# Attention and two expert layers on one core: the first query chunk's blocks go to TensorE's transposes, and the round gets a new order

## Chip, cores and metric

One core of a Trainium2 chip runs the kernel. The metric is device time in microseconds (us) of one execution; smaller is better. The kernel before took 905.91 us, the median of three runs (905.5 to 911.83).

## What is computed

Three layers follow one another. The first is causal attention over 4 batches of 12 heads, 448 tokens, 64 features a head. Then come two layers that send each of the 1792 tokens to one of 8 experts; they are not touched by the change.

```python
scores = scale * np.matmul(q, k.transpose(0, 1, 3, 2))
mask = np.triu(np.ones((seq, seq), dtype=bool), k=1)
scores = np.where(mask, -1000000000.0, scores)
scores = scores - np.max(scores, axis=-1, keepdims=True)
attn = np.exp(scores)
attn = attn / (np.sum(attn, axis=-1, keepdims=True) + 1e-09)
return np.matmul(attn, v).astype(np.float32)
```

## The kernel before

**Tiles.** Attention goes over 24 pairs of heads. The 448 tokens are cut into four chunks of 112 (`CP`), and because of the causal mask query chunk c needs key chunks 0 to c only: 1 + 2 + 3 + 4 = 10 blocks of 112x112 a head (`NB`). For the product with the values a block must stand with its keys on the partitions, so every block of exponentials is transposed.

**Stages of a pair.** `qk` writes the mask and the scores of two query chunks for both heads into four banks of PSUM (`sc`). `rowmax` on DVE finds the maximum of a row (`nm`), `expo` on ACT writes the exponentials to `ex`. Blocks are then split in two halves of 16 bits: `hi` is the block in fp16, `lo` what that leaves over. Two ways lead from there.

- The six blocks of chunks 0, 1 and 2 (`ND`) are split first: `halves_hi` writes `ah` on ACT, `halves_lo` writes `al` on DVE. Then the queue of SP transposes them by DMA into `th` and `tl`, one `DMA_TRANSPOSE` a head and half, four a pair.
- The four blocks of chunk 3 are transposed in fp32 by TensorE into the bank `tb0` (`last_chunk`, one "filling" a head), and split when they are read out of it: ACT writes `ph`, DVE writes `pl`.

`values` multiplies them with the values, which are split in three parts: five products a block, 50 a head, all for one head in a bank `av`, but for one chunk of the second head that goes to `tb1`. `combine` on DVE divides by the sum and writes the result `xb`. `route_t` and `route_l` prepare the choice of experts of the next layer, and a generator of routing steps (`routing`) gives DVE one small step at each `tick`.

**What sets the order.** The program is scheduled by hand: each engine runs its instructions in the order in which the code issues them. The loop over g (L783) is a pipeline; a pass of it, called a round here, works on the scores of pair g, the splits and transposes of pair t = g - 1, the values of pair v = g - 2 and the routing of pair r = g - 3. On the queue of SP a round holds, in this order, the loads of q, k and v of later pairs (L371, L377), two transposes of `tl`, in some rounds a store of `xb`, and two transposes of `th` (all four issued by L421, the helper `transposed`). The transposes of `tl` that a round issues are read by `values` in the next.

In a round TensorE does: scores of chunks 0 and 1, the first filling (head 0), `route_t`, `values(v, 0)`, scores of chunks 2 and 3, the second filling (head 1), `values(v, 1)`, `route_l`.

```python
    boff = [0, 1, 3, 6]
...
    def transposed(dst, src, e):
        nc.sync.dma_start_transpose(dst[:, e * ND * CP : (e + 1) * ND * CP].rearrange("p (n q) -> p n q", q=CP),
                                    src[:, e].rearrange("p n k -> p (n k)"))
```

Of the kernel before, what the change touches and what calls it, by code (L numbers as in the profile page):

```python
# [9 lines left out]
F32 = mybir.dt.float32  # L10
F32R = mybir.dt.float32r
BF16 = mybir.dt.bfloat16
F16 = mybir.dt.float16
# [43 lines left out]
def attention_two_moe_kernel(  # L57
# [258 lines left out]
    NB = NCH * (NCH + 1) // 2  # L316
    ND = NB - NCH
    exs = [at_p.tile([CP, 2, NB, CP], F32, name=f"ex{i}") for i in range(NEX)]
# [4 lines left out]
    phs = [av_p.tile([CP, 2 * NCH * CP + 16], F16, name=f"ph{i}") for i in range(NTP)]  # L323
    pls = [av_p.tile([CP, 2 * NCH * CP + 16], F16, name=f"pl{i}") for i in range(NTP)]
    for t in ahs + als:
        vec.memset(t[:, :, :, CP:], 0.0)
# [5 lines left out]
    for t in phs + pls:  # L332
        vec.memset(t[:, 2 * NCH * CP :], 0.0)


    tb = [ps_t.tile([P, 512], F32, tag="t", name="tb0"), ps_x.tile([P, 512], F32, tag="t2", name="tb1")]

    def side():

        return tb[0][:, S:] if tb else ps_t.tile([P, 512], F32, tag="t", name="t")  # L340

# [49 lines left out]

    boff = [0, 1, 3, 6]
    scs, nms, avs = {}, {}, {}
# [41 lines left out]

    def last_chunk(g, e):

        pt = tb[0][:CP, :S]
        for j in range(NCH):
            pe.transpose(pt[:, j * CP : (j + 1) * CP], exs[g % NEX][:, e, ND + j], ident[:CP, :CP])  # L440
        yield
        ph, pl = (t[g % NTP][:, e * S : (e + 1) * S] for t in (phs, pls))
        act.activation(ph, pt, AF.Copy, scale=ASC)
        yield
        vec.scalar_tensor_tensor(out=pl, in0=pt, scalar=ASC, in1=ph, op0=ALU.mult, op1=ALU.subtract)
        tick()

    VW = HD + 1

    def values(g, e):  # L450

        if e == 1 and g not in tails:
            tails[g] = tb[1][:, S:]
        if e == 0:
            avs[g] = ps_x.tile([P, 512], F32, tag="av", name=f"av{g}")
        v0, v1, v2 = (t[:, e] for t in vss[g])
        for c in range(NCH):
            k = c if e == 0 else NCH + (c - 1) % NCH
            at = k * VW
            for j in range(c + 1):  # L460
                if c < NCH - 1:
                    o = (e * ND + boff[c] + j) * CP
                    hi, lo = (t[g % NTH][:CP, o : o + P] for t in (ths, tls))
                else:
                    o = (e * NCH + j) * CP
                    hi, lo = (t[g % NTP][:, o : o + P] for t in (phs, pls))
                ops = ((hi, v1), (hi, v0), (hi, v2), (lo, v0), (lo, v1))
                for i, (l, r) in enumerate(ops):
                    first, final = j == 0 and i == 0, j == c and i == 4
                    whole = r is v1  # L470
                    if k < 2 * NCH - 1:
                        dst = avs[g][:, at : at + VW] if whole else avs[g][:, at + 1 : at + VW]
                        pe.matmul(dst, lhsT=l, rhs=r[:, j], start=first, stop=final)
                    else:
                        if whole:
                            pe.matmul(avs[g][:, at : at + 1], lhsT=l, rhs=r[:, j, :1], start=first, stop=final)
                        pe.matmul(tails[g], lhsT=l, rhs=r[:, j, 1:] if whole else r[:, j], start=first, stop=final)
# [197 lines left out]
    def both(fn, g, *a, ticks=True):  # L675
        for e in range(2):
            fn(2 * g + e, *a)
            if ticks:
                tick()
# [103 lines left out]
    for g in range(NPR + 3):  # L783
# [12 lines left out]
        if 0 <= v < NPR and v % PB == 0:  # L796
            xbs[v // PB] = xb_p.tile([CP, NCH, D], F32, tag="xb", name=f"xb{v // PB}")
        late = [last_chunk(t, e) if 0 <= t < NPR else iter(()) for e in range(2)]
        if g < NPR:
            qk(g, (0, 1))  # L800
        tick(True)
        if g < NPR:
            for c in range(2):
                both(rowmax, g, c)
                if g == c == 0:
                    both(expo, 0, 0, ticks=False)
                    scale_pair(1, vec)
            for c in range(g == 0, 2):
                both(expo, g, c, ticks=False)
        next(late[0], None)  # L810
        next(late[0], None)
        if 0 <= t < NPR:
            halves_lo(t, (0,))
        next(late[0], None)
        if 0 <= t < NPR:
# [16 lines left out]
        if 0 <= v < NPR:  # L832
            values(v, 0)
        if PB <= r < NPR and r % PB < NCH:
# [8 lines left out]
        if g < NPR:  # L843
            qk(g, (2, 3))
            for c in range(2, NCH):
                both(rowmax, g, c)
        next(late[1], None)
        for c in range(2, NCH):
            if g < NPR:
                both(expo, g, c, ticks=False)  # L850
            next(late[1], None)
        if 0 <= v < NPR:
            values(v, 1)
        if 0 <= r < NPR:
            route_l(r)
        if 0 <= v < NPR:
            combine(v, xbs[v // PB])
        if g < NPR:
            halves_hi(g)
        if g + 2 < NPR:  # L860
            scale_pair(g + 2, pool)
        if g == 0:
# [656 lines left out]
```

## Time and profile before

| what | value |
|---|---|
| median of three runs | 905.91 us |
| the profiled execution | 908.99 us |
| its span, first to last instruction | 907.3 us |
| mean granted TensorE clock | 0.974 of full speed |
| PE busy, share of the span | 848.7 us, 94% |
| DVE busy | 678.2 us, 75% |
| ACT busy | 427.1 us, 47% |
| POOL busy | 399.0 us, 44% |

PE is TensorE's matmuls, PEld its loads of the stationary operand, DVE is VectorE, ACT ScalarE, POOL GpSimd, and SPq the sequencer of SyncE, which issues the DMAs. Shares over the whole span mix three layers with different limits. Attention takes some 250 us at the start, so its stage has to be cut out, and is best cut into rounds. A timeline merges neighbours of one kind: "x4" is four instructions, and the time beside it runs from the first start to the last end. "Idle before" is how long the engine stood in front of an instruction, and behind the arrow is what ended that.

### The profile page before, as it was taken

The page shows a single profiled execution, that of the slowest core. Times are in us where ns is not written, and L with a number is a line of the kernel's source. Part 1 is how long each engine was busy: PE and PEld are TensorE (multiplying, and loading weights), DVE is VectorE, ACT ScalarE, POOL GpSimd, SP SyncE. Part 2 cuts the span into 40 slices and gives each one's busy share as a digit, 9 for nine tenths or more (in the row PEclk, how much of TensorE's full clock was granted, in tenths as well). Part 3 has the DMA queues.
Part 4 walks back from the last instruction along what each step waited for, and adds up shares of the span by engine and source line. Part 5 has one row for each costly group of instructions (what it writes and reads, how often), then busy time and mean ns, then how long its engine had stood idle before and what let it go on. Part 6 is the DMA issues. An engine that isn't in the chain of part 4 may idle for free. (4 is left out here: it accounts for less than half of the span.)

```text
span 907.3 us, 20634 instructions
## 1 busy us (share of the span) xinstructions
PE 848.7 (94%) x6818; PEld 729.4 (80%) x6818; DVE 678.2 (75%) x1782; ACT 427.1 (47%) x777; POOL 399.0 (44%) x433
## 2 busy tenths in 40 slices
PE   5999999988788999999999999999999999999985
PEld 2677776766576899988899989888898898998984
DVE  6888998987876766787747964468786778976783
ACT  4667867775435754575535552245112133221323
POOL 6224245423266264544542564432654544545530
PEclk8899999998799999999999999999999999999997
DMA  7799998998737774687515761120291133511110
GB/s 227 143 160 164 206 199 178 206 174 169 238 97 262 280 260 163 210 290 257 185 46 172 239 229 62 49 73 6 62 328 56 54 108 117 182 43 59 49 38 16
DMA packets 114451, 137.39 MB, mean 151 GB/s; under 512 B 78381, under 2 KB 82787, under 8 KB 114288
## 3 DMA queue, kind: packets, MB, share of 16 engines
q1 hardware_dynamic: 101376, 108.76, 44.4%
q0 software_dynamic: 12912, 26.83, 9.3%
q8 instruction: 57, 0.93, 0.4%
q14 instruction: 106, 0.87, 0.3%
HBM read 101.48 MB, written 19.92 MB: 134 GB/s over the span
## 5 line engine op out<-in xcount | busy, mean ns | idle before, releaser
L748 POOL DMA_INDIRECT xg<-x,xi x128 | 134.4, 1050 | 101.2 <-DMA x<-yb,mg 47.7
L956 PE MATMUL h<-w1h,xh 128*128 128x512 f32 x408 | 164.6, 403 | 2.4 <-issue 1.4
L958 PE MATMUL h<-w1h,xl 128*128 128x512 f32 x408 | 161.1, 395 | 0.9 <-DVE xl L941 0.9
L957 PE MATMUL h<-w1l,xh 128*128 128x512 f32 x408 | 161.2, 395 | 0.7 <-DVE w1l L698 0.7
L1021 PE MATMUL o<-w2h,hh 128*128 128x384 f32 x528 | 137.5, 341 | 0.2 <-issue 0.2
L1021 PE MATMUL o<-w2h,hl 128*128 128x384 f32 x528 | 135.3, 337 | 0.5 <-DVE hl L971 0.5
L1021 PE MATMUL o<-w2l,hh 128*128 128x384 f32 x528 | 134.4, 336 | 0.0
L998 DVE STREAM_TRANSPOSE hs<-h 32x256 f32<-32x256 f32 x240 | 107.1, 446 | 14.3 <-PE h L958 8.5
L418 ACT ACTIVATE ex<-sc,nm 112x112 f32<-112x112 f32 (+1 forms) x192 | 82.8, 499 | 60.9 <-DVE nm L413 58.6
L1021 PEld LDWEIGHTS o<-w2h,hl 128*128 128x128 f32 x528 | 95.3, 188 | 0.8 <-DVE hl L971 0.8
L1021 PEld LDWEIGHTS o<-w2h,hh 128*128 128x128 f32 x528 | 94.0, 188 | 1.8 <-issue 0.4
L1021 PEld LDWEIGHTS o<-w2l,hh 128*128 128x128 f32 x528 | 95.2, 188 | 0.1
L1004 ACT ACTIVATE hh<-hs 128x512 fp32r<-128x512 f32 x30 | 18.4, 631 | 157.7 <-PE o L1021 86.5
L958 PEld LDWEIGHTS h<-w1h,xl 128*128 128x128 f32 x408 | 77.0, 189 | 19.3 <-DVE xl L941 1.6
L956 PEld LDWEIGHTS h<-w1h,xh 128*128 128x128 f32 x408 | 77.2, 189 | 18.8 <-issue 2.3
L957 PEld LDWEIGHTS h<-w1l,xh 128*128 128x128 f32 x408 | 77.3, 189 | 17.9 <-DVE w1l L698 2.6
L413 DVE TENSOR_REDUCE nm<-sc 112x1 f32<-112x112 f32 (+1 forms) x192 | 74.7, 438 | 19.0 <-PE sc L407 18.8
L698 DVE TENSOR_TENSOR w1l<-w1r,w1h 128x1024 fp32r<-128x1024 f32 x66 | 76.4, 1219 | 9.2 <-ACT w1h L696 5.8
L698 DVE TENSOR_TENSOR w2l<-w2r,w2h 128x768 fp32r<-128x768 f32 x78 | 68.8, 951 | 8.6 <-ACT w2h L696 5.6
L407 PE MATMUL sc<-r 64*112 64x112 f32 (+3 forms) x384 | 64.5, 458 | 3.9 <-DVE rt_ren L175 3.9
L696 ACT CAST w1h<-w1r 128x1024 fp32r<-128x1024 f32 x64 | 62.4, 1047 | 9.2 <-PE h L958 5.2
L929 DVE STREAM_TRANSPOSE xr<-xg 128x768 f32<-128x768 f32 x31 | 50.3, 1623 | 17.7 <-DMA xg<-x,xi 11.1
(316 smaller groups left out, 1735.6 us busy)
## 6 DMA issues: line engine op xcount, KB each, us to landing
w1r<-in_w1a SPq DMA_DIRECT2D x48, 512.0 KB
w2r<-in_w2a SPq DMA_DIRECT2D x64, 384.0 KB
r<-in_kqP SPq DMA_DIRECT2D x24, 448.0 KB
w1r<-in_w1b SPq DMA_DIRECT2D x18, 512.0 KB
w2r<-in_w2b SPq DMA_DIRECT2D x24, 384.0 KB
vr<-in_vh SPq DMA_DIRECT2D x24, 224.0 KB
x<-xb SPq DMA_DIRECT2D x16, 336.0 KB
xg<-x,xi POOLq DMA_INDIRECT x128
```

Source lines behind the costliest of these rows:

```text
L407: pe.matmul(scs[2 * g + e, c][:CP, :n], lhsT=r[rs, 1, c * CP : n], rhs=r[rs, 0, :n], start=False, stop=True, skip_group_check=True)
L413: vec.tensor_reduce(out=nms[h][:, c : c + 1], in_=scs[h, c][:CP, : CP * (c + 1)], axis=AX.X, op=ALU.min)
L418: act.activation(dst, scs.pop((h, c))[:CP, :n], AF.Exp, bias=nms[h][:, c : c + 1], scale=-1.0)
L696: act.copy(hi[k], r[k])
L698: vec.tensor_sub(lo[k], r[k], hi[k].bitcast(F32))
L748: pool.indirect_dma_start(out=xgs[j % 3][:, q * (D // Q) : (q + 1) * (D // Q)], out_offset=None, in_=quarters, in_offset=IND(ap=xi[:, q : ...
L929: vec.transpose(xr.rearrange("p k (q r) -> p q k r", q=Q), xgs[j % 3].rearrange("p (q r k) -> p q k r", q=Q, k=KD))
L956: pe.matmul(hps, lhsT=xh[:, c], rhs=w1h[c][:, ns], start=(c == 0), stop=False)
L957: pe.matmul(hps, lhsT=xh[:, c], rhs=w1l[c][:, ns], start=False, stop=False)
L958: pe.matmul(hps, lhsT=xl[:, c], rhs=w1h[c][:, ns], start=False, stop=(c == KD - 1))
L998: vec.transpose(hr[cols, :, rows], hps[rows, q * 256 : (q + 1) * 256].rearrange("p (c k) -> p k c", c=QR))
L1021: pe.matmul(ops[:, n, :384], lhsT=h[f // KH][:, f % KH], rhs=w[f][:, n * 384 : (n + 1) * 384], start=(f == 0 and st == 0), stop=(f == KF - ...
```

## The change

The block of query chunk 0 of each head leaves the DMA's way: `ND` falls from six to five, and the two blocks of a pair (one a head) become a third filling of `tb0`, transposed by TensorE and split out of it into two new small tiles, `qh` (ACT) and `ql` (DVE). `boff` gives the blocks new places, chunks 1 and 2 first, then chunk 0, then chunk 3. `turned_part` takes the place of `last_chunk` and serves all three fillings, and `values` is told which chunks to do and in which order.

The order of a round changes with it:

- The second filling is transposed, copied and split before the scores of chunks 2 and 3 instead of behind them; the third lies behind those scores.
- `values(v, 0)` does chunks 0, 2 and 3 where it stood, and chunk 1 behind the scores of chunks 2 and 3. `values(v, 1)` does chunk 0 last.
- On ACT the copy of the first filling lies between the exponentials of chunk 0 and those of chunk 1.
- `tick(True)` moves from behind the scores of chunks 0 and 1 to behind those of chunks 2 and 3, there is a `tick` more a round, and the routing's small results use the end of `tb1` instead of `tb0`.

```diff
-    ND = NB - NCH
+    ND = NB - NCH - 1
...
+    qhs = [av_p.tile([CP, 2 * CP + 16], F16, name=f"qh{i}") for i in range(NTP)]
+    qls = [av_p.tile([CP, 2 * CP + 16], F16, name=f"ql{i}") for i in range(NTP)]
...
+    for t in qhs + qls:
+        vec.memset(t[:, 2 * CP:], 0.0)
...
-        return tb[0][:, S:] if tb else ps_t.tile([P, 512], F32, tag="t", name="t")
+        return tb[1][:, S:] if tb else ps_t.tile([P, 512], F32, tag="t", name="t")
...
-    boff = [0, 1, 3, 6]
+    boff = [5, 0, 2, 6]
...
-    def last_chunk(g, e):
-
-        pt = tb[0][:CP, :S]
-        for j in range(NCH):
-            pe.transpose(pt[:, j * CP : (j + 1) * CP], exs[g % NEX][:, e, ND + j], ident[:CP, :CP])
-        yield
-        ph, pl = (t[g % NTP][:, e * S : (e + 1) * S] for t in (phs, pls))
+    def turned_part(g, part):
+
+        wide = S if part < 2 else 2 * CP
+        pt = tb[0][:CP, :wide]
+        blocks = [(part, boff[3] + j) for j in range(NCH)] if part < 2 else [(e, boff[0]) for e in range(2)]
+        for k, (e, j) in enumerate(blocks):
+            pe.transpose(pt[:, k * CP : (k + 1) * CP], exs[g % NEX][:, e, j], ident[:CP, :CP])
+        yield
+        at = part * S if part < 2 else 0
+        ph, pl = (t[g % NTP][:, at : at + wide] for t in ((phs, pls) if part < 2 else (qhs, qls)))
         act.activation(ph, pt, AF.Copy, scale=ASC)
         yield
         vec.scalar_tensor_tensor(out=pl, in0=pt, scalar=ASC, in1=ph, op0=ALU.mult, op1=ALU.subtract)
         tick()
+        yield
...
-    def values(g, e):
+    def values(g, e, cs):
...
-        for c in range(NCH):
+        for c in cs:
...
-                if c < NCH - 1:
+                if c in (1, 2):
...
-        tick(True)
-        if g < NPR:
...
-            for c in range(g == 0, 2):
-                both(expo, g, c, ticks=False)
-        next(late[0], None)
-        next(late[0], None)
+            if g:
+                both(expo, g, 0, ticks=False)
+        next(parts[0], None)
+        next(parts[0], None)
+        if g < NPR:
+            both(expo, g, 1, ticks=False)
...
-            values(v, 0)
+            values(v, 0, (0, 2, 3))
+        if v >= 0:
+            drain(parts[1])
...
             qk(g, (2, 3))
+        tick(True)
+        drain(parts[1])
+        if 0 <= v < NPR:
+            values(v, 0, (1,))
+        next(parts[2], None)
+        if g < NPR:
             for c in range(2, NCH):
                 both(rowmax, g, c)
-        next(late[1], None)
-        for c in range(2, NCH):
-            if g < NPR:
-                both(expo, g, c, ticks=False)
-            next(late[1], None)
+            both(expo, g, 2, ticks=False)
+        next(parts[2], None)
+        if g < NPR:
+            both(expo, g, 3, ticks=False)
+        next(parts[2], None)
         if 0 <= v < NPR:
-            values(v, 1)
+            values(v, 1, (1, 2, 3, 0))
```

On PE, in the middle of a round of before, the scores of chunks 2 and 3 (`sc_2`, `sc_3`; one of the four masks is shown) come straight after the last product of `values(v, 0)` with `pl`; the second filling (`tb_253`) comes behind them and in front of `values(v, 1)`:

```order
L473 MATMUL av_1453<-r_236,pl_230 128x65
...
L401 MATMUL sc_2_1504<-mask,identb 128x112
...
L407 MATMUL sc_2_1504<-r_646 112x336
L407 MATMUL sc_2_1506<-r_646 112x336
L407 MATMUL sc_3_1508<-r_646 112x448
L407 MATMUL sc_3_1510<-r_646 112x448
L440 MATMUL tb_253<-ident,ex_215 112x112 x4
L476 LDWEIGHTS th_223
```

Now, at the same place on PE, the second filling (`x4`, into `tb_261`) stands ahead of the scores, and the third (`x2`) behind them and behind chunk 1 of `values(v, 0)`, of which the first and the last product are shown:

```order
L481 MATMUL av_1485<-r_240,pl_230 128x65
L446 MATMUL tb_261<-ident,ex_215 112x112 x4
...
L405 MATMUL sc_2_1532<-mask,identb 128x112
...
L411 MATMUL sc_2_1532<-r_662 112x336
L411 MATMUL sc_2_1534<-r_662 112x336
L411 MATMUL sc_3_1536<-r_662 112x448
L411 MATMUL sc_3_1538<-r_662 112x448
...
L481 MATMUL av_1485<-r_240,th_223 128x65
...
L481 MATMUL av_1485<-r_240,tl_226 128x65
L446 MATMUL tb_261<-ident,ex_215 112x112 x2
```

The second filling has moved ahead by the four masks and the four scores, and two transposes have come in behind these.

On DVE, from the first maximum of a round of before (`nm` from `sc_0`) to the first step of `combine` (`rinv`), there is one pass for `pl` between the two for `al` and one behind the maxima of chunks 2 and 3:

```order
L413 TENSOR_REDUCE nm_860<-sc_1_852 112x1
L431 SCALAR_TENSOR_TENSOR al_220<-ex_216,ah_218 112x6x112
L445 SCALAR_TENSOR_TENSOR pl_230<-tb_253,ph_228 112x448
L431 SCALAR_TENSOR_TENSOR al_220<-ex_216,ah_218 112x6x112
L505 TENSOR_TENSOR xTl_883<-tb_254,xTh_882 128x448
L413 TENSOR_REDUCE nm_858<-sc_2_937 112x1
...
L413 TENSOR_REDUCE nm_860<-sc_3_943 112x1
L445 SCALAR_TENSOR_TENSOR pl_230<-tb_253,ph_228 112x448
L484 TENSOR_SCALAR rinv_1017<-av_886 112x8
```

Now DVE has the second pass for `pl` ahead of those maxima, and the new one for `ql` behind them:

```order
L417 TENSOR_REDUCE nm_880<-sc_1_872 112x1
L435 SCALAR_TENSOR_TENSOR al_220<-ex_216,ah_218 112x5x112
L452 SCALAR_TENSOR_TENSOR pl_230<-tb_261,ph_228 112x448
L435 SCALAR_TENSOR_TENSOR al_220<-ex_216,ah_218 112x5x112
L513 TENSOR_TENSOR xTl_903<-tb_262,xTh_902 128x448
L452 SCALAR_TENSOR_TENSOR pl_230<-tb_261,ph_228 112x448
L417 TENSOR_REDUCE nm_878<-sc_2_953 112x1
...
L417 TENSOR_REDUCE nm_880<-sc_3_959 112x1
L452 SCALAR_TENSOR_TENSOR ql_234<-tb_261,qh_232 112x224
L492 TENSOR_SCALAR rinv_1041<-av_906 112x8
```

The passes for `al` have five blocks instead of six, the second `pl` has moved ahead of four maxima, and a pass over 224 elements has come in.

## Rows read from the trace of the kernel before

**Rows 1.** Rounds: us, busy PE, PEld, DVE, ACT, POOL; clock, DMA share, GB/s.
```profile
68.87:77.71 8.84, 7.83 (x142) 6.05 (x140) 7.44 (x19) 5.88 (x15) 3.27 (x3) 1.00 1.12 168
77.71:85.56 7.85, 7.82 (x141) 6.06 (x140) 7.34 (x19) 5.82 (x14) 3.27 (x3) 1.00 0.95 173
...
126.72:135.64 8.92, 7.97 (x144) 6.27 (x144) 8.43 (x30) 6.32 (x14) 2.39 (x3) 1.00 0.90 156
...
144.12:155.17 11.05, 9.54 (x141) 6.86 (x140) 8.32 (x28) 7.63 (x17) 8.47 (x11) 0.85 1.00 215
...
179.29:190.91 11.62, 9.78 (x145) 7.51 (x144) 8.44 (x28) 6.24 (x14) 2.64 (x3) 0.85 0.98 206
...
199.76:213.00 13.24, 10.91 (x140) 7.69 (x138) 7.87 (x24) 8.48 (x19) 11.28 (x14) 0.74 1.07 218
...
sum 194.02, PE 177.91 PEld 136.54 DVE 169.14 ACT 140.02 POOL 73.80; mean PE 8.09 PEld 6.21 DVE 7.69 ACT 6.36 POOL 3.35
```

**Rows 2.** Timeline of PE in one round: start us, us, instruction.
```profile
95.17 0.59 PE L440 MATMUL tb<-ident,ex 112*112 112x112 f32 x4
95.60 0.55 PE L501 MATMUL tb<-ident,xb 112*128 112x112 f32 x4
95.98 0.19 PE L473 MATMUL av<-r,th 112*128 112x65 bf16 x1
...
97.52 0.36 PE L401 MATMUL sc<-mask,identb 112*128 112x112 bf16 x4
...
99.32 0.59 PE L440 MATMUL tb<-ident,ex 112*112 112x112 f32 x4
99.75 0.17 PE L476 MATMUL av<-r,th 112*128 112x1 bf16 x1
...
101.34 0.36 PE L513 MATMUL lg<-xTh,enT 128*16 128x448 f32 x1
```

**Rows 3.** Waits from 25 to 225 us: us in total, times, longest.
```profile
PEld L473 <- DMA tl<-al: 8.5, 9, 1.8
...
DVE pl L445 <- ACT ph L443: 6.2, 19, 0.9
```

**Rows 4.** Timeline of PE's weight loads: two waits for `tl`.
```profile
72.22 0.11 PEld L473 LDWEIGHTS <-tl 112*128 112x128 f16 x2 [1.13 <-DMA tl<-al]
...
183.90 0.11 PEld L473 LDWEIGHTS <-tl 112*128 112x128 f16 x2 [1.29 <-DMA tl<-al]
```

**Rows 5.** Timeline of SP's queue, one round of DMA issues.
```profile
61.59 3.37 SPq L421 DMA_TRANSPOSE th<-ah  x2
65.07 0.52 SPq L371 DMA_DIRECT2D r<-in_kqP  x1
...
66.15 2.55 SPq L421 DMA_TRANSPOSE tl<-al  x2
```

**Rows 6.** Timeline of DVE in an undisturbed round, and one maximum of a later one.
```profile
78.75 0.21 DVE L492 TENSOR_TENSOR xb<-tb,rinv 112x64 f32<-112x64 f32 x1
78.88 1.04 DVE L413 TENSOR_REDUCE nm<-sc 112x1 f32<-112x112 f32 x4
79.84 0.84 DVE L431 SCALAR_TENSOR_TENSOR al<-ex,ah 112x672 f16<-112x672 f32 x1
80.92 0.62 DVE L445 SCALAR_TENSOR_TENSOR pl<-tb,ph 112x448 f16<-112x448 f32 x1 [0.23 <-ACT ph L443]
81.46 0.85 DVE L431 SCALAR_TENSOR_TENSOR al<-ex,ah 112x672 f16<-112x672 f32 x1
82.22 0.61 DVE L505 TENSOR_TENSOR xTl<-tb,xTh 128x448 fp32r<-128x448 f32 x1
...
94.90 0.26 DVE L413 TENSOR_REDUCE nm<-sc 112x1 f32<-112x112 f32 x1
```

**Rows 7.** Timeline of ACT: the exponentials of chunks 0 and 1.
```profile
79.18 1.28 ACT L418 ACTIVATE ex<-sc,nm 112x112 f32<-112x112 f32 x4
```

**Rows 8.** Busy PE in a stretch of 2 us; granted clock, DMA share, GB/s.
```profile
186.00:188.00 2.00, 2.00 (x14) 0.51 0.70 180
```

More of the change, by code (lines that the diff above doesn't have):

```diff
@@ L446, in last_chunk @@
         tick()
+        yield
     VW = HD + 1
-    def values(g, e):
+    def values(g, e, cs):
         if e == 1 and g not in tails:
             tails[g] = tb[1][:, S:]
-        if e == 0:
+        if g not in avs:
             avs[g] = ps_x.tile([P, 512], F32, tag="av", name=f"av{g}")
         v0, v1, v2 = (t[:, e] for t in vss[g])
-        for c in range(NCH):
+        for c in cs:
             k = c if e == 0 else NCH + (c - 1) % NCH
@@ L464, in values @@
                 else:
-                    o = (e * NCH + j) * CP
-                    hi, lo = (t[g % NTP][:, o : o + P] for t in (phs, pls))
+                    o = (e * (c + 1) + j) * CP
+                    hi, lo = (t[g % NTP][:, o : o + P] for t in ((phs, pls) if c == NCH - 1 else (qhs, qls)))
                 ops = ((hi, v1), (hi, v0), (hi, v2), (lo, v0), (lo, v1))
@@ L797, in attention_two_moe_kernel @@
             xbs[v // PB] = xb_p.tile([CP, NCH, D], F32, tag="xb", name=f"xb{v // PB}")
-        late = [last_chunk(t, e) if 0 <= t < NPR else iter(()) for e in range(2)]
+        parts = [turned_part(t, k) if 0 <= t < NPR else iter(()) for k in range(3)]
         if g < NPR:
             qk(g, (0, 1))
-        tick(True)
-        if g < NPR:
             for c in range(2):
@@ L807, in attention_two_moe_kernel @@
                     scale_pair(1, vec)
-            for c in range(g == 0, 2):
-                both(expo, g, c, ticks=False)
-        next(late[0], None)
-        next(late[0], None)
+            if g:
[4 more added lines that the diff above has]
+            both(expo, g, 1, ticks=False)
         if 0 <= t < NPR:
             halves_lo(t, (0,))
-        next(late[0], None)
+        next(parts[0], None)
         if 0 <= t < NPR:
@@ L857, in attention_two_moe_kernel @@
             combine(v, xbs[v // PB])
+        if g + 2 < NPR:
+            scale_pair(g + 2, pool)
         if g < NPR:
             halves_hi(g)
-        if g + 2 < NPR:
-            scale_pair(g + 2, pool)
         if g == 0:
```

## Prediction

> **What bounds the kernel now.** The change lies in the attention stage, the first 250 us of 907. The first view to read is the busy time of each engine, round by round: a round is what one pass of the loop over pairs does, and I cut the stretches at the start of the first instruction of `combine` on DVE (`rinv`). In [rows 1] an undisturbed round takes 7.85 us and PE is busy for 7.82 of it, DVE for 7.34, ACT for 5.82. So PE is full, and DVE has half a microsecond to spare. The timeline of PE [rows 2] shows it from inside: one group of matmuls starts where the last ends, 95.17 to 101.34, with no idle time noted in front of any. Over the 22 rounds from 34.23 to 228.25 PE is busy for 177.91 of 194.02 us.
>
> The rest is in disturbed rounds. The waits, by who waited for whom, name the largest one on the weight loads of PE: 8.5 us in 9 waits for the transposing DMA of `tl`, the low half of the exponentials [rows 3]. One took 1.13 us at 72.22 [rows 4], and its round, that of 68.87, 8.84 instead of 7.85 [rows 1]. Two rounds are worse. In those of 144.12 and 179.29 PE was busy for 9.54 and 9.78 us with as many matmuls as elsewhere, at a mean granted clock of 0.85: after the wait for `tl` at 183.90 [rows 4] the clock fell to about 0.5, the lower of its two levels (1.2 instead of 2.4 GHz) [rows 8]. The round of 199.76 is the longest, 13.24 us at 0.74; no wait for `tl` stands in it. A third kind of round carries extra small steps on DVE, mostly of the routing: in that of 126.72 DVE is busy for 8.43 of 8.92 us, and there DVE sets the pace. Seven of the 22 rounds have DVE busy for over 8 us.
>
> Why `tl` is late is read from the queue of SP [rows 5]. The two transposes of `th` are issued from 61.59, the loads of the next pair at 65.07 and right behind them, and the two of `tl` from 66.15. These follow one another without a pause, so `tl` leaves when SP has come through the five ahead of it. An issue of a transpose takes 1.28 us (2.55 for two).
>
> **The change part by part.** *TensorE.* Two transposes of 112x112 come in per pair. Four of them move PE on by 0.43 us (99.32 to 99.75 in [rows 2]), so two cost 0.215. The products with the values are as many as before. In 24 pairs that is 5.2 us at most; in seven rounds DVE is the longer engine, so I count 17 x 0.215 = 3.7 us. From below: nothing, if all rounds had idle time to hide it, which [rows 1] excludes for the undisturbed ones.
>
> Here the Trainium skill speaks against the change. [Rows 2] say 0.43 us of PE for four transposes, though the four last 0.59 us from first start to last end, so that one by itself lasts about 0.27 (0.59 - 3 x 0.107). The page "TensorE: Matmul & The Clock Gate", section "Part 4: PE-mode transpose", gives about 275 ns for a transpose of 128x128 inside a kernel, in bf16. If two took that one after the other, 24 pairs would pay an estimated 13.2 us instead of 5.2, and the sum below would come out near the old time plus 4. The row is for this tile and this place, and I go by it.
>
> *DVE.* The low half of the third filling is a pass over 224 elements. The pass over 448 took 0.62 us and the one that reads 64 elements from the same kind of memory 0.21 [rows 6], which is 1.07 ns an element: 0.38 us for 224. Each of the two passes for `al` shrinks from 672 to 560 elements, 0.12 us at that slope. Net +0.14 us a round; it counts where DVE sets the pace: 7 x 0.14 = 1.0 us. Bounds: 7 x (0.21 - 0.24) or nothing, and 24 x 0.38 = 9.1 if DVE set the pace everywhere and `al` did not shrink.
>
> *ScalarE* gains one copy of 224 elements, some 0.43 us if it goes as the four exponentials with 672 elements in 1.28 us [rows 7], and loses 2 x 112 elements of `ah`, as much; with 5.82 busy of 7.85 it has the room. The first copy `ph` now stands behind two of these exponentials instead of four. DVE's `pl` waited 0.23 us for `ph` at 80.92 [rows 6], 6.2 us in 19 waits in all [rows 3]. That goes, but DVE is not what bounds those rounds: I count nothing for it. Were DVE the bound, it would be worth up to 6.2.
>
> *The queue of SP.* Order and number of DMAs stay; each transpose has five blocks of 128 columns instead of six. Whether an issue shrinks with its blocks no row shows. If not at all, `tl` leaves no earlier; if in proportion, by 0.21 us each, and three issues (both of `th`, the first of `tl`) lie before the first `tl` is away: 0.64 us. I take the proportion. On the other side, `values(v, 0)` begins with the chunk that needs no DMA, five products (50 products fill 95.98 to 97.52, 0.031 us each [rows 2]): the need for `tl` comes 0.15 us later. Together 0.8 us, against waits of 0.94 on average (8.5/9). Of the 8.5 us I let 6.0 go. Of the slow clock in two rounds (9.54 + 9.78 - 2 x 7.82 = 3.7 us) I let 3.0 go, since the clock fell there after PE had stood. Bounds: 0 and 12.2 us.
>
> *The new order.* The second filling is transposed before the scores of chunks 2 and 3, no longer behind them. It needs `tb0`, so it waits until DVE's `pl` has read the first filling. By [rows 2] PE comes there 0.43 (first filling) + 0.38 (`route_t`) + 1.24 (40 products) = 2.05 us after the scores of chunks 0 and 1. DVE begins the maxima 0.27 us ahead of that point (94.90 in [rows 6]); 0.96 for four maxima (78.88 to 79.84), 0.64 for the shorter `al` (81.46 to 82.22, less 0.12) and 0.62 for `pl` put its end at 1.95. It just fits. Behind it queue the scores, the third filling and all of `values(v, 1)`. I count nothing, but a routing step on DVE ahead of `pl` is enough to make PE wait. The third filling needs the end of the second `pl`, by the same count about 3.8 us after that point; PE comes there at 2.05 + 0.43 + 1.80 + 0.31 = 4.6. The last 16 columns of four new tiles, cleared at the start, cost DVE less than 0.21 us each (the small pass) and lie under the first loads.
>
> **The sum.** +3.7 + 1.0 - 6.0 - 3.0 = -4.3 us. The profiled execution took 908.99 us (907.3 of span), which gives 904.7; it lies 3.1 above the median of the three runs, 905.91. With the same difference the median becomes 901.6, which I forecast: about half a per cent faster, which a measurement of this kernel can hardly tell from no change (1%, 9.1 us, is what it can tell).
>
> **The rivals.**
> 1. *`tl` is as late as before.* The transfer, not the issue, could set its arrival, or an issue could cost the same for five blocks. For it: `tl` was on its way from 66.15, its two issues were over at 68.70, and PE still waited for it until 72.22. Against: fewer bytes are queued ahead as well. Then only the prices stay: 905.9 + 4.7 = 910.6.
> 2. *The second filling becomes the new wait.* In every round PE stands before the scores of chunks 2 and 3 until DVE has read `tb0`; the scores come late, DVE's maxima with them, and the round grows. For it: the count above leaves 0.10 us, and seven rounds have DVE work in the way. Against: in a longer PE round DVE gets ahead. If `pl` is late by x in 22 rounds, the change is slower than before from x = 0.2 (22 x 0.2 = 4.4 eats the 4.3), and by over 1% from 0.6. At 0.75: 905.9 - 4.3 + 16.5 = 918.1.
> 3. *All disturbances go.* The waits for `tl` fall to nothing (-8.5, -3.7), and the round of 199.76 (13.24 - 7.82 = 5.4) runs like the others, as DMA traffic is lighter. 905.9 + 4.7 - 17.6 = 893.0. For it: these are the same rounds in which much is in flight. Against: no wait for `tl` stands in the longest round.
> 4. *Transposes one after the other.* Standing alone in front of `values(v, 1)`, the two new ones may each take their whole 0.27 us: 24 x 0.54 = 13.0 in place of 3.7, which gives 905.9 - 4.3 + 9.3 = 910.9. [Rows 2] speak against it: the first product starts 0.43 us after the first of four transposes.
>
> **How the numbers follow.** Forecast 0.50; rival 1, 0.15; rival 2, 0.12; rival 3, 0.20; rival 4, 0.03. Faster by over 1% (under 896.9): most of rival 3 (0.17) and the lower edge of the forecast (0.08): 0.25. Slower by over 1% (above 915): most of rival 2 (0.09) and a little of rival 1 (0.02): 0.11. Within: 0.64. The range runs from 891, just below rival 3, to 914, beyond rival 1 and into rival 2. The forecast's own range is 897 to 908.
>
> **What would show it.** Right: undisturbed rounds of 8.0 to 8.1 us with PE full; waits for `tl` under 3 us in total; issues of transposes near 1.06 us; no wait of DVE's first `pl` for `ph`; no lower clock between 34 and 195 us. Wrong: rounds still at 7.8 (the new transposes were hidden), an idle PE ahead of the second filling with DVE's `pl` as what it waited for (rival 2), or transposes still issued in 1.25 us and `tl` as late as before (rival 1).

## The result, and the profile after

The changed kernel took 920.24 us (median of four runs, 915.65 to 922.37) where the kernel before took 906.56 on the same chip: a ratio of 1.0126, 95% interval 1.0086 to 1.0166. (The ratios on record are not quotients of the two medians, which would be 1.015 here; the text goes by the ratios.) It is slower by over one per cent. The prediction said 901.6, within 891 to 914: wrong in sign, and outside its range.

The profiled execution took 918.71 us, its span is 917.0 (before 907.3). I cut it at the same places as before: the first and the last `rinv` of `combine`, and the first product of the first expert layer (`h` from `w1h`).

| stretch | before, us | after, us | difference |
|---|---|---|---|
| start to first `combine` | 34.23 | 38.65 | +4.4 |
| first to last `combine` (23 rounds) | 200.49 | 200.77 | +0.3 |
| last `combine` to the expert layer's first product | 8.52 | 15.48 | +7.0 |
| from there to the end | 664.06 | 662.10 | -2.0 |
| span | 907.3 | 917.0 | +9.7 |

In these two executions the loss lies ahead of the rounds and behind them, and the prediction worked only on the rounds. The transition's loss repeats: 15.40 us in e_second and 15.83 in e_head, two runs further down. The head's size is less sure: with the same first passes the first `combine` starts at 36.16 us in e_late (34.23 before), and at 38.41 in e_gather and 39.30 in e_v3 (38.65 after). The rounds take 197.10 us in e_late, whose code for the rounds is that of before (200.49) but for the gather, so a few us there are no finding.

**The rounds.** The stretches of after, columns as in [rows 1]; the last one is the transition:

```profile
38.65:49.85 11.20, 9.34 (x141) 6.93 (x139) 9.07 (x25) 6.35 (x16) 2.61 (x3) 0.85 0.70 130
49.85:57.86 8.01, 8.01 (x143) 6.29 (x142) 7.33 (x20) 5.91 (x15) 3.13 (x3) 1.00 0.74 141
123.92:135.64 11.72, 10.07 (x147) 7.52 (x146) 9.97 (x28) 6.33 (x16) 5.09 (x6) 0.85 0.93 167
...
206.34:215.15 8.81, 8.21 (x144) 6.31 (x142) 7.43 (x20) 7.58 (x19) 3.47 (x6) 1.00 1.04 213
239.42:254.90 15.48, 4.78 (x26) 2.66 (x23) 7.51 (x25) 2.03 (x5) 3.77 (x4) 0.69 0.63 237
```

An undisturbed round takes 8.01 us with PE busy throughout, 0.16 more than the 7.85 in [rows 1]: the price of two transposes, about as counted. The round that took 13.24 us at a clock of 0.74 in [rows 1] takes 8.81 at full clock. No wait for `tl` stood in that round before; PE stood 2.0 us in four gaps that end with "issue". It runs without them in e_third too (8.41), and why is not known. Others have become long, the first one above all (11.20, before 9.12), and those with routing steps: DVE is busy for 9.97 us in that of 123.92, and over the 23 rounds for 181.28 us, before 174.96. The waits from 25 to 225 us, as in [rows 3]:

```profile
DVE pl L452 <- ACT ph L450: 9.3, 11, 3.8
PEld tb L446 <- DVE pl L452: 9.1, 10, 2.0
PE tb L446 <- DVE pl L452: 7.6, 10, 1.9
PEld L481 <- DMA tl<-al: 5.2, 11, 1.2
```

The waits for `tl` fell from 8.5 to 5.2 us, and a wait of PE for `pl` has come in, 7.6 us in ten places. In the first round one reads how, on DVE and then on PE:

```profile
40.08 1.43 DVE L803 CAST mt<-mod_i 112x4 f32<-112x4 int32 x4
41.42 1.04 DVE L417 TENSOR_REDUCE nm<-sc 112x1 f32<-112x112 f32 x4
42.38 0.73 DVE L435 SCALAR_TENSOR_TENSOR al<-ex,ah 112x560 f16<-112x560 f32 x1
43.03 0.61 DVE L452 SCALAR_TENSOR_TENSOR pl<-tb,ph 112x448 f16<-112x448 f32 x1
```
```profile
43.69 0.95 PE L446 MATMUL tb<-ident,ex 112*112 112x112 f32 x4 [1.86 <-DVE pl L452]
```

Four casts for the routing stand ahead of the maxima (before they stood there as well, but no filling waited for this `pl`), `pl` ends at 43.64, and only then may the second filling go into `tb0`; the scores of chunks 2 and 3 queue behind it. The queue of SP shows the term that failed outright: two issues take 2.51 us with five blocks, 2.55 with six in [rows 5].

```profile
62.94 2.51 SPq L425 DMA_TRANSPOSE tl<-al  x2
```

**The transition.** PE, then POOL, of after:

```profile
253.28 1.54 PE L954 MATMUL xt<-ident,xg 128*128 128x128 f32 x6 [8.26 <-DMA xg<-x,mg]
```
```profile
236.41 1.30 POOL L650 DMA_INDIRECT meta<-mt,r1sir  x1 [0.19 <-issue]
243.09 1.66 POOL L737 DMA_INDIRECT mg<-meta,ld_idxm  x1 [5.38 <-DMA meta<-mt,r1sir]
249.37 0.95 POOL L740 DMA_INDIRECT xg<-x,mg  x1 [4.62 <-DMA mg<-meta,ld_idxm]
```

And POOL of before:

```profile
211.33 1.10 POOL L729 DMA_INDIRECT mg<-meta,ld_idxm  x1 [0.18 <-issue]
214.02 0.95 POOL L732 DMA_INDIRECT xg<-x,mg  x1 [1.58 <-DMA mg<-meta,ld_idxm]
...
236.55 0.95 POOL L642 DMA_INDIRECT meta<-mt,r1sir  x1 [21.47 <-DVE ld_rowm L286]
```

`gather_early` fetches the first tokens of the expert layer in two steps, `mg` and `xg`. Before, POOL issued them at 211 and 214, ahead of the four scatters of batch 2 into `meta`. Now these scatters stand first, the gather of `mg` waits until the last has landed, `xg` waits for `mg`, and PE for `xg`: 8.26 us. The scatters are steps of the routing generator, one step a `tick`, and a pass now has a tick more (in the last passes each counts six times) and the forced one at another place. So on POOL, whose work the change does not name, the order turned round.

**The head.** SP's transposes of the first two pairs, before and then after, and one pass on DVE of after:

```profile
16.57 2.65 SPq L421 DMA_TRANSPOSE th<-ah  x2
...
26.44 2.85 SPq L421 DMA_TRANSPOSE th<-ah  x2
```
```profile
18.60 2.64 SPq L425 DMA_TRANSPOSE th<-ah  x2
...
30.56 3.81 SPq L425 DMA_TRANSPOSE th<-ah  x2
```
```profile
14.72 0.32 DVE L365 CAST enT<-tb 128x48 fp32r<-128x48 f32 x2 [1.73 <-PE tb L362]
...
26.64 0.62 DVE L452 SCALAR_TENSOR_TENSOR pl<-tb,ph 112x448 f16<-112x448 f32 x1 [3.77 <-ACT ph L450]
```

The pipeline is filling here. In the pass g = 0 the moved `tick(True)` puts steps for the expert vectors (`enT`) between the maxima of pair 0. In g = 1, where there are no values yet, the second `pl` stands ahead of the maxima and waits 3.77 us for `ph`. The first pair's transposes leave 2.0 us later, the second's 4.1.

### The profile page after: what moved, and what is told of

The parts are those of the page before. It is cut to its first block, busy times and chain, and to the rows that moved or that the text cites. A ratio compares the mean times of both kernels' runs of the same rounds, so it can differ in the third digit from the quotient of the medians.

```text
span 917.0 us, 20806 instructions
## 1 busy us (share of the span) xinstructions
PE 854.8 (93%) x6866; PEld 737.4 (80%) x6866; DVE 684.0 (75%) x1810; ACT 431.3 (47%) x801; POOL 403.4 (44%) x433
## 5 line engine op out<-in xcount | busy, mean ns | idle before, releaser
L756 POOL DMA_INDIRECT xg<-x,xi x128 | 138.5, 1082 | 100.0 <-DMA x<-yb,mg 45.6
L422 ACT ACTIVATE ex<-sc,nm 112x112 f32<-112x112 f32 (+1 forms) x192 | 85.3, 497 | 38.2 <-DVE nm L417 37.3
```

The costliest lines, as they stand in the source:

```text
L422: act.activation(dst, scs.pop((h, c))[:CP, :n], AF.Exp, bias=nms[h][:, c : c + 1], scale=-1.0)
L756: pool.indirect_dma_start(out=xgs[j % 3][:, q * (D // Q) : (q + 1) * (D // Q)], out_offset=None, in_=quarters, in_offset=IND(ap=xi[:, q : ...
```

## The experiments

Ratios are to the kernel before, run beside each group of runs on the same chip; its median was 908.92 us beside e_gather, e_second and e_order6, 911.64 beside e_head2, e_v3, e_tb1 and e_b3, 911.18 beside e_plfirst, e_casts, e_best and e_late, and 908.25 beside e_nothird, e_third and e_best3. In one profile of each the rounds differ by a few us from run to run, so whole times are judged by the ratios.

| run | median, us | ratio, 95% interval |
|---|---|---|
| e_gather | 913.5 | 1.0044, 1.0016 to 1.0072 |
| e_second | 914.4 | 1.0053, 1.0023 to 1.0082 |
| e_order6 | 919.45 | 1.0118, 1.0064 to 1.0173 |
| e_head2 | 912.63 | 1.0009, 0.9979 to 1.0038 |
| e_v3 | 914.96 | 1.0048, 1.0026 to 1.0071 |
| e_tb1 | 924.19 | 1.014, 1.0113 to 1.0166 |
| e_b3 | 908.57 | 0.9968, 0.9942 to 0.9994 |
| e_plfirst | 911.17 | 1.0013, 0.9982 to 1.0044 |
| e_casts | 911.3 | 1.0007, 0.9982 to 1.0032 |
| e_best | 906.84 | 0.9961, 0.9935 to 0.9986 |
| e_late | 918.76 | 1.0092, 1.0059 to 1.0124 |
| e_nothird | 918.49 | 1.0114, 1.0093 to 1.0135 |
| e_third | 906.84 | 0.9997, 0.9978 to 1.0016 |
| e_best3 | 904.84 | 0.9974, 0.9952 to 0.9996 |

### The order on POOL

**e_gather**

```diff
+        if g == NPR:
+            m1.gather_early((0,), 2 * S)
...
-            m1.gather_early((0,), 2 * S)
```

> The changed kernel with one edit: the early gather of the first tokens of the expert layer is issued at the start of the pass g = 24, so that on POOL it stands ahead of the four scatters of batch 2, as in the kernel before. Theory A (the order on POOL delays the first expert layer): from the last combine to the first product of the expert layer 8 to 9 us instead of 15.5, and the whole about 7 us shorter than the changed kernel, 911 to 915 us. Rival (the gather is late because its data or the weights are): the gather still waits, the stretch stays at 15 us, and the time at 919 to 922.

```profile
218.54 1.11 POOL L737 DMA_INDIRECT mg<-meta,ld_idxm  x1 [0.17 <-issue]
223.67 0.96 POOL L740 DMA_INDIRECT xg<-x,mg  x1 [4.02 <-DMA mg<-meta,ld_idxm]
...
231.18 0.95 POOL L650 DMA_INDIRECT meta<-mt,r1sir  x1 [6.44 <-DVE ld_rowm L286]
```

The gather is ahead of the scatters again, the transition takes 6.65 us (237.74 to 244.39), and the ratio falls from 1.0126 to 1.0044: 0.8 per cent, 7.4 us.

**e_late**, the same in the other direction: the kernel before, with its gather issued two passes later.

```diff
-            m1.gather_early((0,), 2 * S)
...
         if g == NPR + 2:
+            m1.gather_early((0,), 2 * S)
             warm(ps_T, "T", WV)
```

> The kernel before with one edit: the early gather is issued at the pass g = 26, which puts it on POOL behind the four scatters of batch 2, in the order that the changed kernel has. Theory A: from the last combine to the first product of the expert layer 15 us or more instead of 8.5, with TensorE's transposes of xg waiting for the gather, and the whole 6 to 10 us longer than before, a ratio of 1.007 to 1.011. Rival (in the old order of the round POOL gets to the gather in time all the same): within 0.3 per cent of before.

```profile
238.97 1.09 POOL L642 DMA_INDIRECT meta<-mt,r1sir  x1 [0.19 <-issue]
245.06 1.00 POOL L729 DMA_INDIRECT mg<-meta,ld_idxm  x1 [5.01 <-DMA meta<-mt,r1sir]
```
```profile
251.48 1.54 PE L938 MATMUL xt<-ident,xg 128*128 128x128 f32 x6 [11.59 <-DMA xg<-x,mg]
```

Put behind the scatters, the gather costs the kernel before 0.9 per cent, with PE waiting 11.59 us for `xg`. Theory A holds in both directions.

### The head

**e_head** takes the forced `tick(True)` out of g = 0 and puts the second `pl` of g = 1 back; its edit is the second part of e_head2's diff below.

> The changed kernel with the first two passes put back: no forced routing step in the pass g = 0, and in the pass g = 1 the second filling is split behind the maxima of chunks 2 and 3. Theory B (the head of the pipeline lost 4.4 us to these two): first combine at about 34.5 to 36 us instead of 38.65, and the whole 3 to 4 us shorter than the changed kernel, 915 to 918 us. Rival (the head's loss is absorbed later, where the expert layer waits for the gather anyway): first combine earlier by as much, the whole unchanged, 919 to 922.

In this kernel the second filling of g = 1 overwrites in `tb0` the transposed expert vectors before DVE has read them, so the routing works with other vectors; only its time up to the attention's end is used. The first `combine` starts at 35.92 instead of 38.65. **e_head2** keeps the vectors in `tb1` and has e_gather's edit too:

```diff
-        pt = tb[0][:, : KD * E].rearrange("p (c e) -> p c e", e=E)
+        pt = tb[1][:, S : S + KD * E].rearrange("p (c e) -> p c e", e=E)
...
-        tick(True)
-        drain(parts[1])
+        if g:
+            tick(True)
+        late = parts[1] if g == 1 else parts[2]
+        if g != 1:
+            drain(parts[1])
...
-        next(parts[2], None)
+        next(late, None)
...
```

> The changed kernel with the early gather at the start of the pass g = 24 (as in the run e_gather) and the first two passes put back: no forced routing step in g = 0; in g = 1 the second filling is split behind the maxima of chunks 2 and 3; the small transposes of the prepared expert vectors go into the free 64 columns of tb1 in place of tb0. Theory B (these passes cost the head): first combine at 35.5 to 36.5 us instead of 38.4, and the whole 2 to 3 us under e_gather's 913.5, 910 to 912. Rival (the rest of the kernel waits for something that the head does not move): first combine earlier, the whole 913 to 915.

```profile
16.38 2.64 SPq L425 DMA_TRANSPOSE th<-ah  x2
...
27.77 3.46 SPq L425 DMA_TRANSPOSE th<-ah  x2
```

The first transposes leave at 16.38 (before 16.57), the second pair's at 27.77 (before 26.44, after 30.56), the first `combine` starts at 35.40, and the ratio is 1.0009. Against e_v3, run beside it and the same kernel but for the head and one reordering that gave nothing, that is 0.4 per cent less. The two intervals overlap a little, so the earlier start is shown better than its worth in the whole. With gather and head put back, the changed kernel is level with the one before.

### The rounds: what `tl` and `pl` are worth

**e_v3** (on e_gather):

```diff
-            values(v, 0, (0, 2, 3))
+            values(v, 0, (0, 3, 2))
```

> e_gather with one more edit: values(v, 0) takes its chunks in the order 0, 3, 2 instead of 0, 2, 3, so that 25 products that need no DMA stand ahead of the first one that needs tl (0.6 us more). Theory E (tl is late by about half a microsecond a time, and PE pays that): the waits for tl fall from about 5 to under 2 us, the 24 rounds shorten by 3 to 5 us, the whole 908 to 911. Rival (PE then waits as long for something else, pl or the scores): waits for tl go, the rounds stay at 199, the whole 912 to 915.

```profile
PE tb L446 <- DVE pl L452: 8.2, 10, 1.9
...
PEld L481 <- DMA tl<-al: 1.2, 4, 0.4
```

The waits for `tl` go down to 1.2 us, and the time does not move: 1.0048 after 1.0044. The rival held.

**e_plfirst** (on e_head2, with e_v3's order): on DVE the first `pl` ahead of both passes for `al`.

```diff
+        next(parts[0], None)
         if 0 <= t < NPR:
             halves_lo(t, (0,))
-        next(parts[0], None)
-        if 0 <= t < NPR:
             halves_lo(t, (1,))
```

> e_head2 with two more edits: values(v, 0) takes its chunks as 0, 3, 2 (as in e_v3), and on DVE the first pl stands ahead of both passes for al instead of between them, so that tb0 is read about 0.7 us earlier and tl leaves about 0.6 us later. Theory C (PE's waits for pl, 10 us in 11 places in e_head2, lengthen the rounds): they fall to 3 to 5 us, the 24 rounds shorten by 4 to 6 us from 203.8, the whole 0.4 to 0.6 per cent under e_head2, a ratio to before of 0.995 to 0.997. Rival (DVE sets the pace in those rounds, and PE waits at the next place): waits for pl fall, the rounds stay at 202 to 204, the ratio at 1.000 to 1.003.

```profile
PE tb L446 <- DVE pl L452: 5.5, 5, 1.9
```

PE's waits for `pl` fall from 10.0 us in e_head2 to 5.5, the ratio stays (1.0013). The rival again: taking half of this wait away gave no time that shows. Part of it moved: DVE's waits for `ph` grew from 3.9 us in 8 places to 12.9 in 25.

**e_casts** (on e_head2): the casts of the first round are spread over five passes.

```diff
-            vec.tensor_scalar_mul(tau_h, tau_t, 0.5)
-            vec.reciprocal(tau_r, tau_h)
-            for b in range(B):
-                vec.tensor_copy(mts[b][:, :, 3], mod_i[:, b * NCH : (b + 1) * NCH, 0])
...
+        if 4 <= g < 8:
+            vec.tensor_copy(mts[g - 4][:, :, 3], mod_i[:, (g - 4) * NCH : (g - 3) * NCH, 0])
+        if g == 8:
+            vec.tensor_scalar_mul(tau_h, tau_t, 0.5)
+            vec.reciprocal(tau_r, tau_h)
```

> e_head2 with the four small casts and the two passes for tau, which stand on DVE ahead of the maxima of the pass g = 3 (1.7 us there), spread over the passes g = 4 to 8, behind the low halves. Theory C: the round that begins with the first combine, 11.2 us, falls to 8.0 to 9.0, PE's wait of 2 us for pl in it goes, and the other rounds keep their lengths: the whole 2 to 3 us under e_head2, a ratio to before of 0.998. Rival (the first round is long because of the drained routing steps, or what is spread lengthens five rounds): first round 10 to 11, or the sum of the first six rounds unchanged at 52.7; ratio 1.001.

```profile
36.73:44.72 7.99, 7.68 (x141) 6.08 (x139) 7.33 (x20) 5.91 (x15) 3.13 (x3) 1.00 0.67 135
```

The first round falls from 11.20 to 7.99 us, so its excess was the wait behind the casts. The whole is at 1.0007: two to three us were expected, and the interval of 0.25 per cent each way, 2.3 us, can't tell that from nothing.

**e_second** moves the second filling back behind the scores and puts the third between the chunks of `values(v, 1)`.

```diff
-        if v >= 0:
-            drain(parts[1])
...
-        drain(parts[1])
...
-        next(parts[2], None)
+        next(parts[1], None)
...
+        drain(parts[1])
         if 0 <= v < NPR:
-            values(v, 1, (1, 2, 3, 0))
+            values(v, 1, (1, 2, 3))
+        drain(parts[2])
+        if 0 <= v < NPR:
+            values(v, 1, (0,))
```

> The changed kernel with the second filling back behind the scores of chunks 2 and 3, its low half behind their maxima as in the kernel before, and the third filling between the chunks of values(v, 1). Theory C (PE stands before the scores of chunks 2 and 3 until DVE has read the first filling): the waits of PE for pl (9.1 and 7.6 us in the rounds) fall under 4 us together, the 24 rounds take 190 to 196 us instead of 200.8, and the head shortens by about 2 (its g = 1 pass is as before). Whole: 908 to 915. Rival (what PE waits for moves elsewhere: DVE is the longer engine in those rounds): rounds 199 to 202, the whole 917 to 921.

It is faster than the changed kernel: 1.0053 instead of 1.0126, though its gather is as late (transition 15.40 us). The profile accounts for a part only: the first `combine` starts at 36.09, as in e_head, 2.6 us earlier. The waits of PE for `pl` fall from 7.6 to 5.2 us, not under 4, and the rounds do not shorten: 202.15 us, an undisturbed one 8.28 (PE busy for all of it). So the profile speaks against theory C, while the whole time, 914.4 us, lies where that theory put it; whether the place of the second filling costs the rest is not settled.

**e_tb1** goes further: e_v3 with the second filling back as here, without the forced tick in g = 0, the expert vectors in `tb1`, and the third filling into `tb1`, straight behind the second.

```diff
-        pt = tb[0][:CP, :wide]
+        pt = tb[part // 2][:CP, :wide]
...
+        next(parts[1], None)
         next(parts[2], None)
```

> e_v3 with the PE order changed further: the second filling back behind the scores of chunks 2 and 3 with its low half behind their maxima, and the third filling right behind it, in tb1 instead of tb0, so that neither waits for a read of the filling before it; no forced routing step in g = 0. Theory C (PE's wait for pl costs the rounds 7 us, and it comes only from where the fillings stand): waits of PE for pl under 2 us, quiet rounds still 8.0, the 24 rounds 190 to 194 us, first combine at 36, the whole 900 to 906. Rival (in the rounds with routing steps DVE is the longer engine, and PE's wait moves to the scores or the maxima): rounds 196 to 200, the whole 908 to 913.

```profile
PE tb L485 <- DVE ql L452: 20.8, 20, 2.1
```

No wait for `pl` is left, and PE waits about 1 us in every round for DVE's read of `tb1`, since `values(v, 1)` writes its last chunk there. That is 1.4 per cent slower than before, and the form that rival 2 of the prediction had: a new wait in each round.

### The third filling and the order apart

**e_order6** is the changed kernel without the third filling (and without its tick), **e_nothird** is e_head2 without it:

```diff
-    ND = NB - NCH - 1
+    ND = NB - NCH
...
-                if c in (1, 2):
+                if c < NCH - 1:
...
-        parts = [turned_part(t, k) if 0 <= t < NPR else iter(()) for k in range(3)]
+        parts = [turned_part(t, k) if 0 <= t < NPR else iter(()) for k in range(2)] + [iter(())]
```

> The changed kernel without the third filling: six blocks a head go by DMA as before, everything else in the new order. Theory D (the new order costs, the third filling little): head, transition and waits for pl stay as in the changed kernel, quiet rounds 7.8 instead of 8.0, waits for tl 7 to 9 us instead of 5.2, the whole 915 to 921. Rival (the third filling itself is what costs): 904 to 910.

> e_head2 without the third filling: six blocks a head by DMA, the new order of the round otherwise kept, gather and head put back. If the third filling brings what the prediction counted (-4.3 us), this is 4 to 5 us slower than e_head2: ratio to before 1.004 to 1.007, with waits for tl of 8 us or more in place of 2.2. Rival (the third filling is worth nothing, its price and its saving are equal): ratio 0.998 to 1.003.

Of e_order6, POOL:

```profile
224.27 1.10 POOL L737 DMA_INDIRECT mg<-meta,ld_idxm  x1 [0.18 <-issue]
...
244.27 0.95 POOL L650 DMA_INDIRECT meta<-mt,r1sir  x1 [14.89 <-DVE ld_rowm L286]
```

Here the gather is ahead of the scatters without any edit for it, although `tick(True)` stands where the change put it. The tick of the third filling does not turn the order by itself either: e_third, below, has it with `tick(True)` in its old place, and there the gather comes first as well:

```profile
210.72 1.46 POOL L737 DMA_INDIRECT mg<-meta,ld_idxm  x1 [0.17 <-issue]
...
233.12 0.95 POOL L650 DMA_INDIRECT meta<-mt,r1sir  x1 [17.98 <-DVE ld_rowm L286]
```

So it takes the added tick and the new places together. Without that loss the kernel still takes 1.0118, and e_nothird 1.0114, with these waits:

```profile
PE av L481 <- DMA tl<-al: 12.4, 10, 2.6
PEld L481 <- DMA tl<-al: 10.2, 5, 2.7
PE tb L446 <- DVE pl L452: 5.3, 6, 2.0
```

The new order by itself costs 1.1 per cent, and there the third filling brings it all back: from 1.0114 to e_head2's 1.0009, with waits for `tl` of 2.2 us instead of 10.2. That is some 9.5 us with the filling's own price already paid, give or take 3, where the prediction's sum came to 4.3. In the new order a wait for `tl` is also handed on. The second filling follows `values(v, 0)` on PE, and DVE's `pl` of it stands ahead of the maxima; of e_nothird, on PE and then on DVE:

```profile
73.91 0.13 PEld L481 LDWEIGHTS <-tl 112*128 112x128 f16 x2 [2.29 <-DMA tl<-al]
```
```profile
76.26 0.62 DVE L452 SCALAR_TENSOR_TENSOR pl<-tb,ph 112x448 f16<-112x448 f32 x1 [2.06 <-ACT ph L450]
```

Such a wait of DVE follows each of PE's six waits for `tl` of over 1 us there (1.16 us at 107.01 and 0.93 at 109.36, 2.02 at 191.74 and 2.75 at 194.90), whereas in the kernel before no wait of `pl` for `ph` is longer than 0.9 [rows 3]. So one late transfer stops both busy engines. Which of the moves costs how much was not isolated.

**e_third** makes the third filling alone (`turned_part`, `qh`, `ql`, five blocks by DMA), in the order of before. The cut shows where it is put in:

```diff
+        if g > 1:
+            next(late[2], None)
         if g < NPR:
             qk(g, (2, 3))
...
+        if g > 1:
+            drain(late[2])
...
```

> The kernel before with the third filling alone: chunk 0 transposed by TensorE into tb0 ahead of the scores of chunks 2 and 3, its low half ahead of their maxima, five blocks a head by DMA; all else in the old order. If the new order of the rest is what ate the forecast: waits for tl 3 to 5 us, ratio to before 0.993 to 0.997. If the third filling is worth nothing by itself: waits for tl fall as well, but ratio 0.999 to 1.003.

```profile
61.13:69.28 8.15, 8.14 (x144) 6.34 (x142) 7.46 (x20) 6.06 (x16) 3.16 (x3) 1.00 0.64 149
```
```profile
PE tb L446 <- DVE pl L452: 6.8, 8, 1.9
...
PEld L481 <- DMA tl<-al: 2.0, 4, 0.9
```

The waits for `tl` fall from 8.5 to 2.0 us, an undisturbed round grows from 7.85 to 8.15, PE waits 6.8 us for `pl` and 2.1 for `ql`, and the whole is 0.9997, interval 0.9978 to 1.0016. In the old order the third filling is worth nothing that shows.

### A version that beats both

**e_b3** is the kernel before with chunk 3, which needs no DMA, first in `values(v, 0)`; **e_best** spreads the casts as well; **e_best3** adds the third filling to both, with chunk 0, which then needs no DMA either, ahead of chunk 3 (0, 3, 1, 2).

```diff
-        for c in range(NCH):
+        for c in ((3, 0, 1, 2) if e == 0 else range(NCH)):
```

> The kernel before with one edit: values(v, 0) takes chunk 3, which needs no DMA, first (3, 0, 1, 2), so that 20 products stand ahead of the first that needs th or tl. Theory E: the waits for tl fall from 8.5 to under 3 us without any third filling, and the whole is 4 to 8 us under before: 899 to 904 where before gives 907. Rival (the DMA comes so late that 0.6 us does not reach, or the time is lost again): waits stay over 5 us, the whole within 2 us of before.

> The kernel before with chunk 3 first in values(v, 0) (as in e_b3) and the casts and tau spread as in e_casts, no third filling. If both hold: waits for tl 4 to 5 us instead of 8.5, the first round 7.9 to 8.2 instead of 9.1, ratio to before 0.994 to 0.996. Rival (the first round's excess moves to the later ones): ratio 0.997, as e_b3.

> e_third with the chunks of values(v, 0) in the order 0, 3, 1, 2 and the casts and tau spread as in e_best. If the third filling adds to what chunk 3 first gives: ratio under 0.995. If both only cover the same waits for tl, and the filling costs its 0.2 us a round: ratio 0.997 to 1.001, worse than e_best's 0.9961.

The waits for `tl` are 4.2 us in e_b3 and 4.5 in e_best. e_b3 gains 0.3 per cent, e_best 0.4 (906.84 against 911.18 us), intervals below 1. The whole gain of e_b3 was smaller than expected. The third filling does not add: 0.9974 is not under e_best's 0.9961, and the two can't be told apart. e_best is faster than both kernels of this case, by under half a per cent than the one before.

## Why the prediction was wrong

Three steps failed: the cut of the stage, the new order counted at nothing, and the shorter issue as what brings `tl` earlier.

- **The cut.** It said "the change lies in the attention stage" and took 22 rounds from 34.23 to 228.25 us. The head (+4.4) and the transition (+7.0) were in no term and no rival. The runs show both: 0.8 per cent from POOL's order (e_gather, e_late), about 0.4 from the head (e_head2 against e_v3, with the overlap told there). The added `tick` and the moved `tick(True)` were told in the change, and the prediction has a routing step only as DVE work ahead of `pl`, at no price; that a generator gets ahead, and that POOL's scatters are among its steps, was not followed.
- **"The new order. I count nothing."** By e_nothird it costs 1.1 per cent once gather and head are as before. This cancels the saving; the wait for `tl` that goes on to DVE is one way in which it does so.
- **The queue of SP.** "I take the proportion" failed: 1.25 us an issue with five blocks (2.51 for two), not 1.06. `tl` got no earlier start from that, yet its waits fell to 5.2 us, and 2.0 in e_third. What shortens them then is not the issue, and not a quicker transfer either: from issue to landing a transpose of `tl` takes 4.7 us at the median with five blocks (4.6 in e_third), and 4.5 and 4.6 with six (e_nothird, e_order6). The need that comes 0.15 us later would not do it alone. An undisturbed round that is longer by 0.16 to 0.30 us gives `tl` that much more time as well; this is argued, not tested.
- **The saving of 6.0 + 3.0.** In the profile 3.3 of the 6.0 went. The clock was lower in two other rounds now, those of 38.65 and 123.92 at 0.85, the first right behind PE's wait of 1.86 us for `pl`; and it no longer fell in the round that took 13.24. As whole times: some 9.5 us in the new order (e_nothird to e_head2), none in the old (e_third). The 9.5 has the price in it, so there the net saving was over twice the forecast, but against an order that costs as much. That a wait goes is not a gain by itself: e_v3 took nearly all that was left and gained nothing.
- **TensorE and DVE.** Right in size for the single instruction: an undisturbed round grew by 0.16 us where 0.215 was counted (by 0.30 in e_third); `ql` takes 0.38 as worked out (29.07 to 29.45 in the head), `al` 0.73 for 0.72. The sum for DVE was too small: it is busy 6.3 us longer over the 23 rounds where 1.0 was counted, and an undisturbed round has no part in that (7.33, before 7.34), so it lies in the long rounds. The first `pl` hardly waits for `ph` any more, as forecast, but of the 11 waits that are left (9.3 us in all) ten are those of the second `pl` in its new place.
- **Rival 2** came true as a mechanism (PE idle ahead of the second filling, `pl` as what it waits for, DVE steps in the way), with 7.6 us in ten rounds for 16.5 in 22. Its time, 918.1, is near the measured one by luck: gather and head were not in it, and e_plfirst halved the wait and the time stayed. **Rival 4** is out: PE went on 0.22 us after the first of the two transposes in the changed kernel (55.85 to 56.07), just where this rival put them. The Trainium skill's price, about 275 ns for one transpose of 128x128 in bf16 inside a kernel ("TensorE: Matmul & The Clock Gate", section "Part 4: PE-mode transpose"), does not add up by the piece here: this row, of 112x112 in fp32, has 0.22 us for two. The 13.2 us that the prediction estimated from that price were set against 5.2, but its sum holds 3.7, so the result would have been the old time plus 5, not plus 4.

```profile
55.85 0.38 PE L446 MATMUL tb<-ident,ex 112*112 112x112 f32 x2
56.07 0.19 PE L481 MATMUL av<-r,th 112*128 112x65 bf16 x1
```

## What to carry to other kernels

Where a generator hands out steps by ticks, an added or moved tick can reorder every engine that a step touches: compare the whole program order of each engine, to the end of the stage, and look for what moved past an early load or gather. Price the first passes of a pipeline and the stage behind it as rows of their own, not only the steady rounds. And before work is moved off a DMA that is late, try to use its result later: chunk 3 first adds no instruction and its interval lies below 1 (0.9942 to 0.9994), which that of the third filling in the old order does not (0.9978 to 1.0016), though the two overlap.

## What the runs showed of the hardware

The issue of a transposing DMA on SP took 1.25 us with five blocks of 128 columns and 1.28 with six (half of 2.51 and 2.55); over all 48 transposes of `tl` the median is 1.22 and 1.23. Of the gather behind the scatters one sees the chain in the changed kernel: 5.38 us of waiting for the scatters to land, from the issue of `mg` (243.09) to that of `xg` 6.28, and from there to PE's start 3.91.

In one execution an earlier start did not become a shorter time. In e_b3's profile the expert layer's first product starts at 238.83 us instead of 243.24, but from 280 to 290 us the granted clock is 0.78, where before had 1.00; the span came out 1.4 us longer than that of before. That the clock is the reason was not tested. Of e_b3, then of before (PE busy, clock, DMA share, GB/s):

```profile
280.00:290.00 10.00, 10.00 (x34) 0.78 0.83 284
```
```profile
280.00:290.00 10.00, 9.16 (x44) 1.00 0.62 183
```
